# Chunked linear attention feeding a SiLU MLP: the recurrence of the tiled chunks goes from steps of 128 tokens to steps of 64

## The chip, the cores and the metric

One core of one Trainium2 chip. The metric is the device time of one execution in microseconds (us); three runs of the kernel before gave 206.91, 207.03 and 207.21, median 207.03 us. Profile times are counted from the start of the profiled span.

## The reference, cut to what matters

Four batches, eight heads, 768 tokens, head size 64. Attention without softmax and with a decay per head, computed block by block of 64 tokens with a running 64x64 state per head; its output, as 3072 rows of 512, goes through a two-layer MLP with a SiLU.

```
for b in range(nb):                       # blocks of 64 tokens
    intra = (qb @ kb.T * Dmask) @ vb      # Dmask: lam ** (i - j), 0 above the diagonal
    inter = (qb * lam ** (pos + 1)) @ kv_state
    out[b] = intra + inter
    kv_state = lam ** 64 * kv_state + (kb * lam ** (63 - pos)).T @ vb
...
h = x @ w_in                              # x: 3072 x 512, w_in: 512 x 2048
out = (h * sigmoid(h)) @ w_out            # w_out: 2048 x 512
```

The kernel doesn't keep the decay in the state: q is multiplied by a power of lambda, k by its inverse (tables `lam_fwd`, `lam_bwd` by position in the sequence), so that the state is a plain sum and the mask is 0 or 1. The sum may then be cut into blocks of any size.

## The kernel before, in words

**Chunks, pairs, groups.** The 3072 tokens are 24 chunks of 128, six to a batch (`NB`). Heads go in four pairs p of two heads j. Two chunks make a group of 256 columns for the MLP; there are 12 groups. Chunks 0 to 5 (batch 0) are done by other code, in the first 49 us, which the change doesn't touch. Chunks 6 to 23 go through `section`, which is called 12 times, between pieces of the MLP.

**What a section does.** `section(outs, scores, states, ...)` computes, for three lists of chunks, in one burst on TensorE: the *outputs* (score times v, name `op<-ss,vb`, and state times q, `op<-qt,kvs`), the *scores* (`sp<-qt,kn`) and the *states* (`kv_ps<-vb,kb`). Every product is 64x64 weights on one quarter of the array. The quarter, or tile, is (r, x): rows half r (which half of the contraction: tokens 0 to 63 or 64 to 127 of a chunk, or one head of the pair) and columns half x (which half of the output's partitions). For outputs, x is set by `at[p]`, which says for each pair whether its two heads lie straight or crosswise.

Because a chunk is 128 tokens and causal, the products with the first 64 keys have 128 moving columns (queries 0 to 127), those with the last 64 keys have 64. State times q has 128 columns, the state products 64.

**The order within a section** is made by a small list planner at L491-L562: a FIFO of products for each of the four tiles, in which a 64-column product is counted at 32 and a 128-column one at 56, and the emitted order is that of the planned start. FIFOs of row half 0: out of pairs 0-1, scores, states, out of pairs 2-3; of row half 1: states, out of pairs 2-3, scores, out of pairs 0-1. Two row halves may not write one PSUM bank at once, so each bank has a leading row half (`leads`, L539), and the other one starts `LAG` = 220 after the leader's last product there, behind a semaphore (L554-L558). Here "turn" means that hand-over.

After the products: output copies PSUM to `xt` (VectorE or ScalarE), masking of the scores (VectorE, L579: two row ranges times two heads for each chunk, so 4 instructions a chunk), and per chunk of states one addition into `total` and one cast to `kvs` (VectorE, L588, L589).

**Order on the engines.** Nothing is rescheduled: each engine executes its instructions in the order in which the Python code emits them. Before a chunk's v can be used, ScalarE casts it to bf16 (`vcast`, `vb<-vf`, L185), in the same queue as the SiLU of the MLP (L610). POOL scales q and k (`scaled`, L355), SP's queue loads and transposes them.

**Where the 12 sections stand** (main loop, L801-L830). An MLP group g has 8 units of the first product (`ffn1_two`, PSUM tag `h`, 2 banks, one SiLU each) and 8 units of the second (`downs`). Section 1 (score of chunk 6) comes before unit 2 of group 2, right behind `vcast(6)`. Sections 2 and 4 (groups 2 and 3) come before unit 6 of the first product. Sections 3 and 5 to 12 come before unit 6 of the second product of groups 2 to 10. Sections 5 to 11 compute scores of two chunks, sections 6 to 12 outputs of two. `vcast(d)`, for the second chunk d of the next group, comes in unit 1 of the second product when g < 4.

| section | first start, us | outs | scores | states |
|---|---|---|---|---|
| 1 | 51.02 | - | 6 | - |
| 2 | 55.04 | 6 | 7 | 6 |
| 3 | 62.85 | 7 | 8 | 7 |
| 4 | 70.77 | 8 | 9 | 8 |
| 5 | 78.63 | 9 | 10, 11 | 9, 10 |
| 6 | 93.80 | 10, 11 | 12, 13 | 12 |
| 7 | 109.11 | 12, 13 | 14, 15 | 13, 14 |
| 8 | 124.43 | 14, 15 | 16, 17 | 15, 16 |
| 9 | 139.86 | 16, 17 | 18, 19 | 18 |
| 10 | 155.17 | 18, 19 | 20, 21 | 19, 20 |
| 11 | 170.49 | 20, 21 | 22, 23 | 21, 22 |
| 12 | 185.90 | 22, 23 | - | - |

The last chunk of a batch (11, 17, 23) needs no state, and the first one (6, 12, 18) reads none.

Of the kernel before, what the change touches and what calls it, by code (L numbers as in the profile page):

```python
# [7 lines left out]
F32 = mybir.dt.float32  # L8
BF16 = mybir.dt.bfloat16
AF = mybir.ActivationFunctionType  # L10
AL = mybir.AluOpType

BLK = 128
# [25 lines left out]
def kernel(  # L39
# [10 lines left out]
    nc = tc.nc  # L50
    B, H, S, D = q.shape
    assert (B, H, S, D) == (4, 8, 768, 64)
    NB = S // BLK
# [150 lines left out]
    cell = {}  # L204
# [150 lines left out]
    def scaled(c, raw, table, name):  # L355
        dst = nat.tile([128, NP, 2, D], BF16, name=name, tag=name, bufs=6 if name == "kb" else 4)
        src, by = raw.pop(c).rearrange("s (p j) d -> s p j d", j=2), decay(table, c % NB)
        if c < NPAD:
            nc.gpsimd.tensor_tensor(dst, src, by, op=AL.mult)
            return dst  # L360
        nc.gpsimd.tensor_tensor(dst[:, :3], src[:, :3, ::-1, :], by[:, :3, ::-1, :], op=AL.mult)  # L361
        nc.gpsimd.tensor_tensor(dst[:, 3:], src[:, 3:], by[:, 3:], op=AL.mult)
        return dst

    def prep_k(c):
# [115 lines left out]

    at = [(1, 0), (1, 0), (1, 0), (0, 1)]
    LAG = 220

    def section(outs=(), scores=(), states=(), e="AA", tags=(("att", 3),) * 2, spare=None):

        jobs = {(r, x): [] for r in range(2) for x in range(2)}  # L491

        def add(r, x, key, lhsT, rhs, dst, start=False):
            jobs[r, x].append((key, rhs.shape[-1], lhsT, rhs, dst, start))

        n = len(outs)
        if outs:
            ops = [psum.tile([128, 2, n, BLK], F32, name="op", tag=t, bufs=b, padded_shape=[128, 2, 2, BLK]) for t, b in tags]
        states = [c for c in states if c % NB < NB - 1]
        if states:  # L500
            kv = psum.tile([128, len(states), NP, D], F32, name="kv_ps", tag="kv", bufs=1, padded_shape=[128, 2, NP, D])
        sps = {}
        for c in scores:
            for j in range(2):
                t, b = spare if spare and not sps else ("att", 3)
                sps[c, j] = psum.tile([128, NP, BLK], F32, name="sp", tag=t, bufs=b)

        def out(r, i):
            first = {0, 1} if r == i else set()
            for w, c in enumerate(outs):  # L510
                vb, qt = natb[c][2], tr[c][0]
                for p in (2 * i, 2 * i + 1):
                    for j in range(2):
                        x = at[p][j]
                        add(r, x, i, vb[half[r], p, x, :], st[c][j][half[r], p, 64 * r:], ops[i][half[x], p % 2, w, 64 * r:], x in first)
                        first.discard(x)
                    if c % NB:
                        x = at[p][r]
                        add(r, x, i, kvb[c][half[r], p, :], qt[half[r], p, :], ops[i][half[x], p % 2, w, :])

        def state(r):
            for w, c in enumerate(states):
                kb, vb = natb[c][1:]
                for p in range(NP):
                    for j in range(2):
                        add(r, j, "kv", kb[half[r], p, j, :], vb[half[r], p, at[p][j], :], kv[half[j], w, p, :],
                            r == 1 and w == 0 and p == 0)

        def score(r):
            for c in scores:  # L530
                qs, kt = tr[c]
                for p in range(NP):
                    for h in range(2):
                        add(r, h, "s", kt[half[r], p, half[h]], qs[half[r], p, 64 * h:], sps[c, r][half[h], p, 64 * h:], True)

        out(0, 0), score(0), state(0), out(0, 1)
        state(1), out(1, 1), score(1), out(1, 0)

        leads = {"kv": 1, 0: 0, 1: 1}  # L539
        free, done, last = {k: 0.0 for k in jobs}, {}, {}  # L540

        def begin(k):
# [7 lines left out]
        while any(jobs.values()):  # L550
            k = min((k for k in jobs if jobs[k]), key=lambda k: (begin(k), k))
            t = begin(k)
            key, cols, lhsT, rhs, dst, start = jobs[k].pop(0)
            if leads.get(key, k[0]) != k[0] and key in last:  # L554
                turn = nc.tensor.nop()
                tc.add_manual_dep(turn.ins, last.pop(key).ins.name,
                                  mybir.DependencyInfo(mybir.DependencyClass.Sync, mybir.DependencyReason.DATA),
                                  reason="row tiles of one bank")  # L558
            ins = nc.tensor.matmul(dst, lhsT=lhsT, rhs=rhs, start=start, stop=True, skip_group_check=True)  # L559
            free[k] = t + (32 if cols == 64 else 56)  # L560
            if leads.get(key) == k[0]:
                done[key], last[key] = max(free[k], done.get(key, 0)), ins  # L562

        def copy_out():
            for w, c in enumerate(outs):
                x = new_xt(c)
            if n == 2:
                x = xt[group_of[c][0]]
            for i, op in enumerate(ops):
                move(e[i], x[:, 2 * i:2 * i + 2, :], op.rearrange("d p w s -> d p (w s)"))  # L570

        if outs:
            copy_out()
        for c in scores:
            st[c] = [work.tile([128, NP, BLK], BF16, name="ss", tag="ss") for j in range(2)]
            for rows, cols in ((half[0], half[0]), (slice(0, 128), half[1])):
                m = mask[rows, cols]
                for j, ss in enumerate(st[c]):
                    nc.vector.tensor_tensor(ss[rows, :, cols], sps[c, j][rows, :, cols],  # L579
                                            m[:, None, :].to_broadcast([m.shape[0], NP, 64]), op=AL.mult)  # L580
        for w, c in enumerate(states):
            b = c // NB
            kvs = nat.tile([128, NP, D], BF16, name="kvs", tag="kvs", bufs=4)
            if c % NB == 0:
                total[b] = nat.tile([128, NP, D], F32, name="total", tag="total", bufs=2)
                nc.vector.tensor_copy(total[b], kv[:, w])
            else:
                nc.vector.tensor_tensor(total[b], total[b], kv[:, w], op=AL.add)  # L588
            nc.vector.tensor_copy(kvs, total[b])  # L589
            kvb[c + 1] = kvs  # L590

    total = {}

    gt = {}
# [203 lines left out]
    def other():  # L798
        return f"o{1 - otag[0]}", 1

    for g in range(2, len(GROUPS) - 1):  # L801
        c, d, a, b = range(2 * g + 2, 2 * g + 6)
        for i in range(8):
            if g == 2 and i == 2:
                vcast(6)
                section((), (6,))
            if g == 2 and i == 4:
                prep_t(9)
                load_next(2)
            if g < 4 and i == 6:  # L810
                section((c,), (d,), (c,), "DD", (("att", 3), other()))
            ffn1_two(g, i)
        for i, unit in enumerate(downs(g)):
            if i == 1:
                vcast(d) if g < 4 else None
                vcast(a)
            if i == 2:
                if g > 2:
# [4 lines left out]
                vcast(b)  # L823
            if i == 6:
                if g == 2:
                    section((d,), (a,), (d,), "AA", (("att", 3), other()))
                else:
                    cs = [x for x in (a, b) if x < NCHUNK]
                    section((d,) if g == 3 else (c, d), cs, (d, a) if cs else (d,), "AD", (("h", 2),) * 2, other())
            ffn2(*unit)  # L830
    g = len(GROUPS) - 1
    for i in range(8):
# [34 lines left out]
```

## Time and profile before

| what | value |
|---|---|
| median of three runs | 207.03 us (206.91 to 207.21) |
| the profiled execution's own time | 207.43 us |
| its span, first to last instruction | 205.7 us |
| TensorE busy | 197.1 us, 96% of the span |
| VectorE, ScalarE, POOL busy | 86.3, 88.1, 54.7 us |
| tiled products of sections (L559) | 936, busy 14.04 us in all |
| DMA | 38.64 MB, mean 188 GB/s |

"Busy" of TensorE is the union of its instructions' times, and a product's time includes the passage through the array, so that a dense stream overlaps itself: a 128x512 product is shown with 379 ns while the next starts 216 ns after it. Starts are what to compare. Some matmul records are missing (346 of the second product's 368 at L643): in the timeline the first one behind a section is, where eight weight loads stand beside seven products.

### The profile page before, as it was taken

The numbers are of one execution on the slowest core, as the hardware profiler recorded it, in microseconds if no ns is written. First come the engines' busy times: TensorE is split into PE (matmuls) and PEld (weight loads), VectorE is DVE, ScalarE is ACT, GpSimd is POOL, SyncE is SP. The second block draws the span as 40 slices with busy tenths as digits, with TensorE's granted clock in tenths as the row PEclk, the third lists the DMA queues.
The fourth block names the chain that finished last, engine by engine and source line by source line (L and its number), as shares of the span: only waits on it lengthen the run. The fifth ranks groups of instructions, "written<-read, shape, count | busy, mean of one in ns | idle before, by whom it ended". The sixth has DMA issues, their size and how long they took to land.

```text
span 205.7 us, 5525 instructions
## 1 busy us (share of the span) xinstructions
PE 197.1 (96%) x2331; PEld 132.5 (64%) x2354; DVE 86.3 (42%) x202; ACT 88.1 (43%) x159; POOL 54.7 (27%) x96
## 2 busy tenths in 40 slices
PE   7789999999999999999999999999999999999994
PEld 2457544567856855856856856856856856856854
DVE  3898557384446055505405514515315415412011
ACT  2677673323642650641641641641641641621610
POOL 5270001744634507606606063161000000000000
PEclk9999999999999999999999999999999999999999
DMA  3999999998959769969949696999998101101102
GB/s 95 332 353 389 394 407 285 326 223 178 275 110 212 168 127 250 188 154 212 200 99 270 102 267 131 137 285 103 391 197 285 51 0 54 54 0 53 54 0 102
DMA packets 95577, 38.64 MB, mean 188 GB/s; under 512 B 80960, under 2 KB 88512, under 8 KB 95552
## 3 DMA queue, kind: packets, MB, share of 16 engines
q1 hardware_dynamic: 92288, 37.50, 72.1%
q10 hardware_dynamic: 3264, 0.79, 1.8%
q8 instruction: 18, 0.29, 0.6%
q14 instruction: 7, 0.06, 0.1%
HBM read 27.27 MB, written 6.29 MB: 163 GB/s over the span
## 4 chain that ended last, share of the span: by engine, by line
PE 92%; SPq 2%; DMA 2%; issue 1%; POOL 1%; DVE 0%
PE o_ps L643 38%; PE h_ps L605 36%; PE h_ps L699 5%; PE op L559 4%; SPq L231 2%; DMA pair<-in_k_dram 2%; PE sp L559 2%; PE o_part L663 2%; PE kv_ps L559 1%; PE kv_ps L337 1%; PE op L317 1%; PE op L478 1%; POOL kp L260 1%; PE sp L452 0%; PE op L312 0%
## 5 line engine op out<-in xcount | busy, mean ns | idle before, releaser
L643 PE MATMUL o_ps<-w_out_bf,g 128*128 128x512 bf16 x346 | 80.7, 379 | 2.1 <-issue 1.4
L605 PE MATMUL h_ps<-xt,w_in_bf 128*128 128x256 bf16 x672 | 75.9, 273 | 0.0
L605 PEld LDWEIGHTS <-w_in_bf 128*128 128x128 bf16 x672 | 65.5, 98 | 10.1
L610 ACT ACTIVATE g<-h_ps 128x512 bf16<-128x512 f32 x84 | 49.8, 597 | 42.1 <-PE h_ps L605 42.0
L643 PEld LDWEIGHTS <-g 128*128 128x128 bf16 x368 | 35.0, 98 | 38.2
L361 POOL TENSOR_TENSOR qb<-qf,lam_fwd 128x384 bf16<-128x384 f32 x18 | 14.9, 828 | 50.8 <-DMA qf<-in_q_dram 39.4
L185 ACT ACTIVATE xt<-op 128x256 bf16<-128x256 f32 (+1 forms) x16 | 7.7, 504 | 44.8 <-issue 24.8
L649 DVE COPY ob<-o_ps 128x512 f32<-128x512 f32 x11 | 7.6, 688 | 46.0 <-PE o_ps L643 46.0
L579 DVE TENSOR_TENSOR ss<-sp,mask 64x256 bf16<-64x256 f32 (+1 forms) x72 | 24.7, 405 | 2.9 <-PE sp L559 2.9
L189 DVE CAST xt<-op 128x256 bf16<-128x256 f32 (+1 forms) x14 | 7.7, 558 | 27.5 <-PE op L559 27.5
L649 DVE COPY pair<-o_ps 128x512 f32<-128x512 f32 x12 | 8.2, 687 | 21.1 <-PE o_ps L643 20.7
L361 POOL TENSOR_TENSOR kb<-kf,lam_bwd 128x384 bf16<-128x384 f32 x18 | 14.9, 829 | 7.0 <-DMA kn<-kb 4.9
L559 PE MATMUL op<-ss,vb 64*64 64x64 bf16 (+1 forms) x288 | 12.5, 207 | 0.0
L559 PEld LDWEIGHTS <-vb 64*64 64x64 bf16 x288 | 9.4, 108 | 4.3 <-issue 4.2
L699 PE MATMUL h_ps<-xt,w_in_bf 128*128 128x512 bf16 x48 | 10.5, 379 | 0.0
L185 ACT ACTIVATE vb<-vf 128x512 bf16<-128x512 f32 x18 | 10.3, 621 | 0.0
L559 PE MATMUL op<-qt,kvs 64*64 64x128 bf16 x120 | 9.2, 218 | 0.0
L699 PEld LDWEIGHTS <-w_in_bf 128*128 128x128 bf16 x48 | 4.7, 97 | 5.5
L708 ACT ACTIVATE g<-h_ps 128x512 bf16<-128x512 f32 x12 | 6.5, 596 | 3.4 <-PE h_ps L699 3.4
L559 PE MATMUL sp<-qt,kn 64*64 64x128 bf16 (+1 forms) x288 | 7.9, 206 | 0.0
L559 PE MATMUL kv_ps<-vb,kb 64*64 64x64 bf16 x240 | 7.8, 195 | 0.0
L352 POOL TENSOR_TENSOR qb<-pair,lam_fwd 128x512 bf16<-128x512 f32 x2 | 2.0, 1042 | 20.0 <-DMA pair<-in_q_dram 20.0
(91 smaller groups left out, 142.8 us busy)
## 6 DMA issues: line engine op xcount, KB each, us to landing
kf<-in_k_dram SPq DMA_DIRECT2D x19, 256.0 KB, 4.3
vf<-in_v_dram SPq DMA_DIRECT2D x19, 256.0 KB, 4.5
qf<-in_q_dram SPq DMA_DIRECT2D x17, 256.0 KB, 4.2
pair<-in_moe_w_out_dram SPq DMA_DIRECT2D x8, 512.0 KB, 8.0
pair<-in_moe_w_in_dram SPq DMA_DIRECT2D x6, 512.0 KB, 7.4
out_dram<-pair SPq DMA_DIRECT2D x12, 256.0 KB, 3.2
out_dram<-ob SPq DMA_DIRECT2D x11, 256.0 KB, 2.0
pair<-in_k_dram SPq DMA_DIRECT2D x4, 256.0 KB, 4.7
```

Of the source, the lines that this page charges most:

```text
L185: nc.scalar.activation(dst, src, AF.Copy)
L189: nc.vector.tensor_copy(dst, src)
L231: nc.sync.dma_start(out=dst[c][:, lo:hi].rearrange("p h r d -> p h (r d)"), in_=src[b, lo:hi, blk * BLK:(blk + 2) * BLK, :].rearrange("h ( ...
L361: nc.gpsimd.tensor_tensor(dst[:, :3], src[:, :3, ::-1, :], by[:, :3, ::-1, :], op=AL.mult)
L559: ins = nc.tensor.matmul(dst, lhsT=lhsT, rhs=rhs, start=start, stop=True, skip_group_check=True)
L579: nc.vector.tensor_tensor(ss[rows, :, cols], sps[c, j][rows, :, cols], m[:, None, :].to_broadcast([m.shape[0], NP, 64]), op=AL.mult)
L605: nc.tensor.matmul(hps[g, i][:, a:a + 256], lhsT=w_in_bf[:, ko, m * 128:(m + 1) * 128], rhs=xt[g][:, ko, :], start=(ko == 0 and u == 0), s ...
L610: nc.scalar.activation(gg.rearrange("p u n -> p (u n)"), hps[g, i], AF.Silu)
L643: nc.tensor.matmul(o, lhsT=gt[g, ko][:, mt * BLK:(mt + 1) * BLK], rhs=w_out_bf[:, ko, :], start=(ko == 0), stop=(ko == KO_OUT - 1))
L649: nc.vector.tensor_copy(ob, o)
L699: nc.tensor.matmul(hps["m", m], lhsT=w_in_bf[:, ko, m * 128:(m + 1) * 128], rhs=xall[0][:, :, ko, :], start=(ko == 0), stop=(ko == KO_IN - 1))
L708: nc.scalar.activation(gg, hps["m", m], AF.Silu)
```

## The change

It affects `section`, its call sites, and the split of POOL's scaling.

- **Half chunks.** The states argument becomes a list of (chunk, half). Each half of 64 tokens adds to the running sum by itself, and each half's queries read the sum as it stood before that half (`kvh[c, h]`). So a score or score-times-v product covers one half against itself only: all of them have 64 columns. State times q becomes two products of 64 columns. The number of products goes from 936 to 1104: 168 more, all of the two kinds that touch the state.
- **Which states when.** `steps` gives a section the halves up to the first half of the last chunk that it scores: section 1 has (6,0), section 2 (6,1) and (7,0), section 3 (7,1) and (8,0), section 4 (8,1) and (9,0), section 5 (9,1) (10,0) (10,1) (11,0), and so on; second halves of the last chunk of a batch are dropped. Before, a section had the states of its output chunk and the one behind.
- **Banks.** Scores of two chunks share one bank per row half (two banks instead of four). With two halves of the same parity, the states of the two row halves get a bank each and need no turn; with fewer they share one, with a turn.
- **Crosswise pairs.** `at` becomes crosswise in pairs 0 and 2 and straight in 1 and 3, and POOL's scaling is split by even and odd pairs instead of the first three and the last.
- **VectorE.** One mask instruction per row half for all scores of a section (two instead of 4 or 8); an addition and a cast for each half (33 instead of 15 of each); two copies of a 64-column mask in section 1.
- **Casts.** `vcast(d)` moves from the second product to just ahead of sections 2 and 4.

```diff
-        nc.gpsimd.tensor_tensor(dst[:, :3], src[:, :3, ::-1, :], by[:, :3, ::-1, :], op=AL.mult)
-        nc.gpsimd.tensor_tensor(dst[:, 3:], src[:, 3:], by[:, 3:], op=AL.mult)
+        nc.gpsimd.tensor_tensor(dst[:, 0::2], src[:, 0::2, ::-1, :], by[:, 0::2, ::-1, :], op=AL.mult)
+        nc.gpsimd.tensor_tensor(dst[:, 1::2], src[:, 1::2], by[:, 1::2], op=AL.mult)
...
-    at = [(1, 0), (1, 0), (1, 0), (0, 1)]
+    at = [(1, 0), (0, 1), (1, 0), (0, 1)]
...
+        states = [(c, h) for c, h in states if (c + 1) % NB or not h]
+        ns = max([sum(h == x for _, h in states) for x in range(2)])
+        shared = ns < 2
+        if scores:
+            sps = [more("sp", [128, len(scores), NP, D]) for _ in range(2)]
         if states:
-            kv = psum.tile([128, len(states), NP, D], F32, name="kv_ps", tag="kv", bufs=1, padded_shape=[128, 2, NP, D])
+            kv = [psum.tile([128, 2, NP, D], F32, name="kv_ps", tag="kv", bufs=1)]
+            if not shared:
+                kv.append(more("kv_ps", [128, 2, NP, D]))
...
-                        add(r, x, i, vb[half[r], p, x, :], st[c][j][half[r], p, 64 * r:], ops[i][half[x], p % 2, w, 64 * r:], x in first)
+                        add(r, x, i, vb[half[r], p, x, :], st[c][j][half[r], p, :], ops[i][half[x], p % 2, w, half[r]], x in first)
                         first.discard(x)
-                    if c % NB:
-                        x = at[p][r]
-                        add(r, x, i, kvb[c][half[r], p, :], qt[half[r], p, :], ops[i][half[x], p % 2, w, :])
+                for h in range(2):
+                    if (c, h) in kvh:
+                        for p in ps:
+                            x = at[p][r]
+                            add(r, x, i, kvh[c, h][half[r], p, :], qt[half[r], p, half[h]], ops[i][half[x], p % 2, w, half[h]])
...
-                        add(r, h, "s", kt[half[r], p, half[h]], qs[half[r], p, 64 * h:], sps[c, r][half[h], p, 64 * h:], True)
+                        add(r, h, f"s{r}", kt[half[r], p, half[h]], qs[half[r], p, half[h]], sps[r][half[h], w, p, :], True)
...
+    def steps(*cs):
+        return [(c, h) for c, h in [(cs[0] - 1, 1)] + [(c, h) for c in cs for h in range(2)] if c > 5][:-1]
...
             if g == 2 and i == 2:
                 vcast(6)
-                section((), (6,))
+                section((), (6,), steps(6))
...
             if g < 4 and i == 6:
-                section((c,), (d,), (c,), "DD", (("att", 3), other()))
+                vcast(d)
+                section((c,), (d,), steps(d), "DD", (("att", 3), other()))
...
             if i == 1:
-                vcast(d) if g < 4 else None
                 vcast(a)
...
                 if g == 2:
-                    section((d,), (a,), (d,), "AA", (("att", 3), other()))
+                    section((d,), (a,), steps(a), "AA", (("att", 3), other()))
...
-                    section((d,) if g == 3 else (c, d), cs, (d, a) if cs else (d,), "AD", (("h", 2),) * 2, other())
+                    section((d,) if g == 3 else (c, d), cs, steps(*cs) if cs else (), "AD", (("h", 2),) * 2, other())
```

## The prediction

> **What bounds the kernel now.** I read the page's busy times and its chain first, then the waits with TensorE as the waiting engine, then the timeline of one section, last ScalarE's timeline around sections 1, 2 and 4.
>
> ```profile
> span 205.7 us, 5525 instructions
> PE 197.1 (96%) x2331; PEld 132.5 (64%) x2354; DVE 86.3 (42%) x202; ACT 88.1 (43%) x159; POOL 54.7 (27%) x96
> PEclk9999999999999999999999999999999999999999
> PE o_ps L643 38%; PE h_ps L605 36%; PE h_ps L699 5%; PE op L559 4%; SPq L231 2%; DMA pair<-in_k_dram 2%; PE sp L559 2%; PE o_part L663 2%; PE kv_ps L559 1%; PE kv_ps L337 1%; PE op L317 1%; PE op L478 1%; POOL kp L260 1%; PE sp L452 0%; PE op L312 0%
> ```
> ```profile
> PE o_ps L643 <- issue: 1.4, 9, 0.2
> PE warm_ps L213 <- DVE zero L119: 1.3, 1, 1.3
> PE tk L276 <- DVE kp L189: 1.1, 1, 1.1
> ```
> TensorE is the chain, at full granted clock, and after the first 16 us it waits for no other engine. The nine 0.16 us of "issue" lie behind sections 3 and 5 to 12, where the first dense product has no record, and are no wait. So each nanosecond that a section's burst takes more or less is a nanosecond of the end, and a new wait of TensorE counts in full.
>
> **What a section costs.** Section 8, TensorE's timeline:
>
> ```profile
> 124.44 0.25 PE L559 MATMUL kv_ps<-vb,kb 64*64 64x64 bf16 x4
> 124.52 0.23 PE L559 MATMUL kv_ps<-vb,kb 64*64 64x64 bf16 x4
> 124.59 0.23 PE L559 MATMUL kv_ps<-vb,kb 64*64 64x64 bf16 x4
> ...
> 124.68 0.22 PE L559 MATMUL sp<-qt,kn 64*64 64x128 bf16 x1
> 124.74 0.22 PE L559 MATMUL sp<-qt,kn 64*64 64x128 bf16 x1
> 124.79 0.22 PE L559 MATMUL sp<-qt,kn 64*64 64x128 bf16 x1
> 124.85 0.22 PE L559 MATMUL sp<-qt,kn 64*64 64x128 bf16 x1
> ...
> 126.09 1.67 PE L643 MATMUL o_ps<-w_out_bf,g 128*128 128x512 bf16 x7 [0.16 <-issue]
> ```
> The four scores are one tile's, 56 ns apart. Each row of four states is two products on each of two tiles, so 32 ns a step and tile (124.52 to 124.59 for two). The four tiles run beside each other. A section therefore lasts as long as its busiest tile: the sum of 56s and 32s in it. Check, busiest tile before, less its last step, plus 24 ns that the first step is always longer (80 instead of 56): section 7 1208 - 56 + 24 = 1176, first to last start measured 1178; section 8 1264, measured 1280; section 11 1264, measured 1261; sections 5, 6 and 9 come 57, 31 and 30 ns above. The mean excess of sections 5 to 11 is 19 ns. From the last start to the next dense product it is 148 ns where that is recorded (sections 2 and 4); the last product has 128 columns, and I take 124 with 64.
>
> **Part 1: all tiled products at 64 columns, crosswise pairs alternating.** Steps for one tile after, all 32 ns: a chunk's scores 4, score times v 4, state times q 2 per half, a half's states 4 on the two tiles of its row half. Before, the three equal pairs of `at` gave tiles (0,1) and (1,0) three of four state-times-q products of 56; now all are even. Two-chunk section 8: 8 + 8 + 8 + 8 steps = 1024, where the busiest tile had 1296. Turns cost nothing there: bank 0's leader ends at 256 and bank 1's at 512, the followers start at 768, over 220 behind. Sections 2 to 4 share a state bank: leader done at 128, follower not before 348, though its scores are done at 256 (224 in section 2); a restart after an idle turn costs 20 more (first steps of 52 instead of 32 in section 3). Section 12 has 256 + 220 + 256 = 732 and 44 of restarts, as now (planned last start 964, measured 1008).
>
> | section | busiest tile before | last start measured | busiest after, with turns | last start after | saved, with 24 of the exit |
> |---|---|---|---|---|---|
> | 3 | 648 | 673 | 604 | 616 | 81 |
> | 5 | 1000 | 1025 | 768 | 760 | 289 |
> | 6, 9 | 1168 | 1167, 1166 | 1024 | 1016 | 175, 174 |
> | 7, 10 | 1208 | 1178, 1178 | 960 | 952 | 250, 250 |
> | 8, 11 | 1296 | 1280, 1261 | 1024 | 1016 | 288, 269 |
> | 12 | 784 | 1008 | 732 | 744 | 288 |
>
> Sum 2.06 us; less 7 times the 19 ns excess 1.93 us. The trace has no stretch with all four tiles at 64 columns, which asks for a start each 8.0 ns. Counted over the trace's starts, the best 16 successive ones are 7.9 ns apart on average, the best 32 8.9, the best 64 9.6; all of these have a tile with 128 columns among them, so they needn't be a limit. Bounds: 8.0, nothing more; 9.6, sections 5 to 11 with 96, 120, 120, 128, 120, 120, 128 products take 1.26 us more. I take 8.0, since the 16 show it.
>
> A rule speaks against this part: the Trainium skill, "TensorE: Matmul & The Clock Gate", section "Wait — 56ns, not 53.3ns?", says that start-to-start of matmuls never falls below about 25 ns, however few columns. The rows above show 7.9 ns across tiles, and 32 on one tile; taken across tiles, the rule would make section 8 last 128 x 25 = 3.2 us, an estimate from that page, and the change cost over 10 us; I go by the rows.
>
> **Part 2: states earlier, a new wait in three sections.** Before, a section's states were of a chunk whose v had been cast long ago. Now sections 1, 2 and 4 have states of chunk 6, 7 and 9, and the cast stands just ahead of them in ScalarE's queue, behind the SiLU of the MLP unit that TensorE has only just finished.
>
> ```profile
> 49.63 1.13 ACTq L239 DMA_DIRECT2D vf<-in_v_dram  x1
> 50.81 1.09 ACT L610 ACTIVATE g<-h_ps 128x512 bf16<-128x512 f32 x2 [1.70 <-PE h_ps L605]
> 51.78 0.63 ACT L185 ACTIVATE vb<-vf 128x512 bf16<-128x512 f32 x1
> ...
> 55.15 0.60 ACT L610 ACTIVATE g<-h_ps 128x512 bf16<-128x512 f32 x1 [0.28 <-PE h_ps L605]
> ...
> 70.88 0.60 ACT L610 ACTIVATE g<-h_ps 128x512 bf16<-128x512 f32 x1 [0.22 <-PE h_ps L605]
> ```
> TensorE's starts follow the emitted order to a few ns in every section, so what is emitted behind a waiting product waits too.
> - Section 1 starts at 51.02; its states come after 4 steps of scores, at 51.17. Chunk 6's cast already runs at 51.78 to 52.41 (two SiLUs are late behind a DMA issue). Release 49 ns later (the SiLU that ends at 51.407 lets a product go at 51.456), four state steps 0.12, exit 0.12: next dense product at 52.70, measured 51.456. **+1.25 us.**
> - Section 2, T = 55.04: the SiLU of unit 5 runs from T + 0.11 to T + 0.70, the cast starts 0.1 before a predecessor's end (51.78 against 51.90) and takes 0.62 to 0.63: release at T + 1.28. The states of (7,0) were due at about T + 0.42. Behind them still 4 + 3 steps less one (0.21) and the exit 0.12: T + 1.615, before T + 0.78. **+0.83 us.**
> - Section 4, T = 70.77: the same, with 4 + 4 steps: T + 1.65, before T + 0.82. **+0.83 us.**
>
> Sum +2.91 us. What queues behind is the rest of the MLP, which has no slack. The landing of v is not late (chunks 6, 7, 9 landed at 45.1, 48.3, 58.5), nor is POOL's k (48.8 and 58.9 for 7 and 9). A pause of 1.1 us (the third row of waits) left the granted clock at full, so I add nothing for it. Bounds: 0 if the casts came in time, 2.91 + 0.3 if the restarts after such a pause are slower. In sections 3 and 5 to 11 the casts come before: they run at 119.85 for section 8, at 124.43.
>
> **Part 3: the rest, at nothing.** VectorE: after section 8 now 0.69 (xt) + 8 x 0.34 (masks) + 2 x 0.77; after, 0.69 + 2 x 0.69 (as the 128x512 masks at L457, 686 ns) + 4 x 0.77 = 5.2 us, with 15 us to the next section; the output copy behind it is 0.3 us later, its bank is wanted 7 us after the section. In section 1 two small mask copies, two masks and the state's copy and cast, some 2 us, end before section 2. xt is copied first as now, 0.8 us before the MLP wants it (126.8 against 127.6). POOL: 828 + 402 ns become two of 128x256, between these 0.6 each; bounds 2 x 0.40 and 2 x 0.83, and POOL scales a chunk over 5 us before its section. Fewer score banks: none is short. If the covers failed, TensorE would wait up to some 0.3 us a section.
>
> **Sum.** +2.91 - 1.93 = +0.98 us: 207.43 becomes 208.4 us for the profiled execution. That lies 0.40 above the median; for the median 207.03 + 0.98 = **208.0 us**.
>
> **Rivals.**
> - *The casts don't hold TensorE up* (faster). Then sections 1, 2 and 4 change by +0.03, -0.07 and -0.08, and the time is 207.03 - 1.93 - 0.12 = 205.0. The point: `vb` must be ready by T + 0.42 in sections 2 and 4. For it speaks ScalarE's idle 0.28 us before each SiLU, and that v landed 7 us before; against it, that a cast emitted after unit 5 can't start before that unit's SiLU, which itself ends at T + 0.70. Chance 8%.
> - *Starts can't come each 8 ns* (slower). At 9.6 ns: 208.0 + 1.26 = 209.3. For it: averages rise with the length of the stretch; against: 7.9 over 16. 14%.
> - *Waits half as long* (no change): one of the three casts earlier, or excesses gone: +0.4 or less, 207.4. 12%.
> - *The bursts don't shrink at all*, turns or LDWEIGHTS taking over: 207.03 + 2.9 = 209.9. For it nothing but that no row shows it; 4%.
>
> Forecast 62%. Measurement tells 0.2% (0.41 us) from no change. Faster 8%, within 12%, slower 80% (forecast, second and last rival). The range leaves out the faster rival, the last one and the far end of the others: 207.3 to 209.3.
>
> **What would show it.** In the profile after: TensorE waits for ScalarE three times, 0.8 to 1.3 us, at sections 1, 2 and 4; sections 5 to 11 last 0.76 to 1.05 us from first to last start; 1104 tiled products. Wrong if no wait on ScalarE appears (205), or if section 8 lasts 1.2 us or more (209).

## The result and the profile after

The kernel after takes 209.45 us (median of six runs, 209.24 to 211.27), the kernel before 207.23 in the same job (six runs, 206.91 to 207.86). The ratio is 1.0119, 95% interval 1.0081 to 1.0158: slower by about 1.2%, and beyond the upper end of the prediction's range. Ratios here and below leave out single runs that took over 1.5% longer than the fastest of their kernel. The profiled execution takes 209.37 us, 1.94 more than the one of before.

The page of after: span, busy times, clock, the chain by line.

```profile
span 207.5 us, 5877 instructions
PE 198.4 (96%) x2522; PEld 131.8 (64%) x2522; DVE 88.0 (42%) x190; ACT 88.2 (42%) x159; POOL 54.9 (26%) x96
PEclk9999999999999999999999999999999999999999
PE 90%; DMA 2%; ACT 2%; SPq 2%; ACTq 1%; POOL 1%; issue 0%; DVE 0%
```

And its waits of TensorE: us in total, times, the longest.

```profile
PE kv_ps L580 <- ACT vb L185: 3.1, 3, 1.6
PE warm_ps L213 <- DVE zero L119: 1.3, 1, 1.3
PE tk L276 <- POOL kp L260: 0.8, 1, 0.8
```

The first line is new: in three sections the state products (the tiled line is now L580) wait for the cast of v. ScalarE and its issuing queue (ACTq) stand in the chain now; before, it read

```profile
PE 92%; SPq 2%; DMA 2%; issue 1%; POOL 1%; DVE 0%
```

The clock is granted in full, so the difference is time that TensorE stood still or spent otherwise, not a slower clock.

Section by section, from first start to the next dense product (148 ns behind the last start before, from the sections where that product has a record; 125 to 143 after, where all have one), the spans differ like this:

| sections | predicted, us | measured, us |
|---|---|---|
| 1, 2, 4: waits | +1.25, +0.83, +0.83 = +2.91 | +1.25, +0.83, +0.82 = +2.90 |
| 3 | -0.08 | +0.04 |
| 5, 8, 11 | -0.29, -0.29, -0.27 | -0.19, -0.15, -0.21 |
| 6, 9 | -0.18, -0.17 | -0.08, -0.02 |
| 7, 10 | -0.25, -0.25 | -0.14, -0.07 |
| 12 | -0.29 | -0.25 |
| bursts, sum | -1.93 (2.06 less the excess of 0.13) | -1.07 |
| all | +0.98 | +1.83 (span: 207.5 - 205.7) |

For section 1 the number is when the next dense product starts (52.70 against 51.456). The section itself began 0.50 us earlier than before, at 50.52, and the wait swallowed that: counted from its own start it lost 1.74.

So one half of the sum came out to 0.01 us and the other half is 0.86 us short. The sections add up to the difference of the spans, so nothing is left for the dense work around them. Another 0.1 lies around the span. The medians differ by 2.2 and the profiled executions by 1.9; the remaining 0.3 has no place in one profile. And 0.2 of the distance to the forecast of 208.0 is its base: it was added to 207.03, and the kernel before takes 207.23 here.

**Where the waits come from.** ScalarE's timeline of after around sections 1 and 2: start, duration, instruction, in brackets the idle time before it.

```profile
49.24 1.52 ACTq L239 DMA_DIRECT2D vf<-in_v_dram  x1
50.81 1.08 ACT L635 ACTIVATE g<-h_ps 128x512 bf16<-128x512 f32 x2 [2.19 <-PE h_ps L630]
51.78 0.63 ACT L185 ACTIVATE vb<-vf 128x512 bf16<-128x512 f32 x1
...
56.41 0.60 ACT L635 ACTIVATE g<-h_ps 128x512 bf16<-128x512 f32 x1 [0.28 <-PE h_ps L630]
56.90 0.62 ACT L185 ACTIVATE vb<-vf 128x512 bf16<-128x512 f32 x1
```

TensorE's timeline of section 2, which starts at 56.30:

```profile
56.55 0.29 PE L580 MATMUL sp<-qt,kn 64*64 64x64 bf16 x8
57.57 0.22 PE L580 MATMUL kv_ps<-vb,kb 64*64 64x64 bf16 x2 [0.73 <-ACT vb L185]
...
57.91 0.50 PE L630 MATMUL h_ps<-xt,w_in_bf 128*128 128x256 bf16 x3
```

The cast starts when the SiLU ahead of it has all but ended and ends at 57.52; the states of chunk 7 start at 57.57, 1.27 after the section's start (predicted 1.28). In section 1 the cast runs at 51.78 to 52.41, as before: the wait is the length by which TensorE is ahead of it.

**Where the bursts are long.** Section 8 of after, TensorE's timeline; each line with x2 is two products, on the two tiles of one row half, so two such lines are a round of the four tiles:

```profile
127.16 0.20 PE L580 MATMUL kv_ps<-vb,kb 64*64 64x64 bf16 x2
127.19 0.20 PE L580 MATMUL op<-qt,kvs 64*64 64x64 bf16 x2
127.19 0.20 PE L580 MATMUL kv_ps<-vb,kb 64*64 64x64 bf16 x2
127.22 0.20 PE L580 MATMUL op<-qt,kvs 64*64 64x64 bf16 x2
127.22 0.20 PE L580 MATMUL kv_ps<-vb,kb 64*64 64x64 bf16 x2
...
127.52 0.20 PE L580 MATMUL kv_ps<-vb,kb 64*64 64x64 bf16 x2
127.54 0.20 PE L580 MATMUL sp<-qt,kn 64*64 64x64 bf16 x2
127.56 0.20 PE L580 MATMUL kv_ps<-vb,kb 64*64 64x64 bf16 x2
127.57 0.20 PE L580 MATMUL sp<-qt,kn 64*64 64x64 bf16 x2
127.59 0.20 PE L580 MATMUL kv_ps<-vb,kb 64*64 64x64 bf16 x2
...
128.04 0.28 PE L580 MATMUL op<-qt,kvs 64*64 64x64 bf16 x8
128.25 0.61 PE L668 MATMUL o_ps<-w_out_bf,g 128*128 128x512 bf16 x2
```

At first the lines of one row half are 32 ns apart (127.16, 127.19, 127.22), later 33 to 34 (127.52, 127.56, 127.59). Around the two turns, at products 95 and 100 (counted from 0), a start comes 17 and 26 ns after the one before instead of 8; so it does, 16 to 18 and 25 ns after, at products 47 and 52 and at 109 and 114, where there is no turn. The last start comes 1.136 us after the first, where the plan had 0.992 and the prediction, with the longer first step, 1.016. The second half of the experiments is about the reason.

### The profile page after: what moved, and what is told of

Same layout as the page of the kernel before. It is cut to its first block, busy times and chain, and to the rows that moved or that the text cites. A ratio compares the mean times of both kernels' runs of the same rounds, so it can differ in the third digit from the quotient of the medians.

```text
span 207.5 us, 5877 instructions
## 1 busy us (share of the span) xinstructions
PE 198.4 (96%) x2522; PEld 131.8 (64%) x2522; DVE 88.0 (42%) x190; ACT 88.2 (42%) x159; POOL 54.9 (26%) x96
## 4 chain that ended last, share of the span: by engine, by line
PE 90%; DMA 2%; ACT 2%; SPq 2%; ACTq 1%; POOL 1%; issue 0%; DVE 0%
PE o_ps L668 38%; PE h_ps L630 35%; PE h_ps L724 5%; PE op L580 3%; DMA pair<-in_k_dram 2%; SPq L231 2%; PE o_part L688 2%; PE kv_ps L580 1%; PE sp L580 1%; ACT g L635 1%; ACTq L239 1%; PE kv_ps L337 1%; ACT vb L185 1%; PE op L317 1%; PE op L478 1%; POOL kp L260 1%
## 5 line engine op out<-in xcount | busy, mean ns | idle before, releaser
L668 PE MATMUL o_ps<-w_out_bf,g 128*128 128x512 bf16 x368 | 83.9, 379 | 0.0
L630 PEld LDWEIGHTS <-w_in_bf 128*128 128x128 bf16 x672 | 65.4, 98 | 10.0
L635 ACT ACTIVATE g<-h_ps 128x512 bf16<-128x512 f32 x84 | 49.8, 597 | 43.9 <-PE h_ps L630 43.9
L361 POOL TENSOR_TENSOR qb<-qf,lam_fwd 128x256 bf16<-128x256 f32 x18 | 11.1, 615 | 53.6 <-DMA qf<-in_q_dram 33.5
L361 POOL TENSOR_TENSOR kb<-kf,lam_bwd 128x256 bf16<-128x256 f32 x18 | 11.1, 615 | 7.2 <-PE kv_ps L580 6.3
L600 DVE TENSOR_TENSOR ss<-sp,mask 128x512 bf16<-128x512 f32 (+1 forms) x22 | 11.9, 584 | 2.4 <-PE op L580 1.4
L612 DVE TENSOR_TENSOR total<-total,kv_ps 128x256 f32<-128x256 f32 x30 | 12.5, 418 | 0.8
L613 DVE CAST kvs<-total 128x256 bf16<-128x256 f32 x33 | 11.2, 339 | 1.1
L580 PE MATMUL kv_ps<-vb,kb 64*64 64x64 bf16 x264 | 8.3, 196 | 3.1 <-ACT vb L185 3.1
L362 POOL TENSOR_TENSOR kb<-kf,lam_bwd 128x256 bf16<-128x256 f32 x18 | 11.2, 624 | 0.0
L362 POOL TENSOR_TENSOR qb<-qf,lam_fwd 128x256 bf16<-128x256 f32 x18 | 11.1, 618 | 0.0
L580 PEld LDWEIGHTS <-vb 64*64 64x64 bf16 x288 | 7.4, 105 | 4.4 <-issue 4.2
L580 PE MATMUL op<-ss,vb 64*64 64x64 bf16 x288 | 9.9, 198 | 0.1
L580 PE MATMUL op<-qt,kvs 64*64 64x64 bf16 x264 | 9.5, 194 | 0.0
```

The costliest lines, as they stand in the source:

```text
L361: nc.gpsimd.tensor_tensor(dst[:, 0::2], src[:, 0::2, ::-1, :], by[:, 0::2, ::-1, :], op=AL.mult)
L362: nc.gpsimd.tensor_tensor(dst[:, 1::2], src[:, 1::2], by[:, 1::2], op=AL.mult)
L600: nc.vector.tensor_tensor(ss, sp.rearrange("k w p q -> k (w p) q"), cell["m"][:, None, :].to_broadcast([128, len(scores) * NP, D]), op=AL. ...
L612: nc.vector.tensor_tensor(total[b], total[b], place(c, h), op=AL.add)
L630: nc.tensor.matmul(hps[g, i][:, a:a + 256], lhsT=w_in_bf[:, ko, m * 128:(m + 1) * 128], rhs=xt[g][:, ko, :], start=(ko == 0 and u == 0), s ...
L635: nc.scalar.activation(gg.rearrange("p u n -> p (u n)"), hps[g, i], AF.Silu)
```

## Experiments

Theory: the waits are the casts' place ahead of sections 2 and 4 and behind ScalarE's DMA issue in section 1, and cost 2.9 us; the bursts save half of what was counted because TensorE can't start a product each 8.0 ns for that long, and because turns aren't free. Rivals: the bursts' dense work around them became slower; the step of a tile is more than 32 ns; the bank of the states or the planner's numbers hold the bursts up; the pauses come from elsewhere.

### The casts on VectorE, earlier

Kernel after, with the casts of v for chunks 6, 7 and 9 taken off ScalarE's queue and emitted one or two units earlier:

```diff
+            if g == 2 and i == 1:
+                vcast(6, "D")
+            if g < 4 and i == 4:
+                vcast(d, "D")
             if g == 2 and i == 2:
-                vcast(6)
...
-                vcast(d)
```

> The kernel after, with the casts of v of chunks 6, 7 and 9 on VectorE one or two MLP units earlier (VectorE is idle there). Theory (three waits on ScalarE's cast cost 1.25 + 0.83 + 0.82 = 2.90 us and nothing else was lost): no wait of TensorE on a cast; sections 1, 2 and 4 last about as long as before (within 0.05 us each), sections 5 to 12 as in the kernel after; some 1.0 us faster than the kernel before, 206.2 against 207.2. Rival (TensorE would wait for something else there, such as masks, state sums or SiLU): at least one of sections 1, 2, 4 keeps 0.3 us or more, and the time is 207 or above.

Measured: 207.03 us (12 runs) against 207.49 (29 runs), ratio 0.9977, 0.9958 to 0.9995. The profiled execution takes 206.57, span 204.9. Its waits:

```profile
PE o_ps L668 <- issue: 1.5, 9, 0.2
PE warm_ps L213 <- DVE zero L119: 1.3, 1, 1.3
PE tk L276 <- POOL kp L260: 0.8, 1, 0.8
```

No cast is waited for (the first line is the missing records again). TensorE's last product starts at 201.38, 3.18 us earlier than in after (204.56); the span is only 2.7 shorter, because the last output is issued on SP's queue for longer in this execution (1.73 us for the last two instead of 1.24). Sections 2 and 4 last 0.702 and 0.781 us from first to last start, instead of 1.486 and 1.518. Three casts moved by one or two units take back the whole loss; what is left of the change is a gain of about 0.2%. Sections 5 to 11 last 0.843, 1.107, 1.060, 1.135, 1.081, 1.108 and 1.075 us: within 1 ns of after but for sections 9 and 10, which had 1.170 and 1.127 there, so the missing half of the saving has nothing to do with the casts.

### The casts on ScalarE, earlier

The same, but on ScalarE:

```diff
+            if g == 2 and i == 1:
+                vcast(6)
+            if g < 4 and i == 4:
+                vcast(d)
             if g == 2 and i == 2:
-                vcast(6)
...
-                vcast(d)
```

> The kernel after, with the same three casts left on ScalarE, but emitted one unit (chunk 6) or two units (7 and 9) earlier. Theory (the place in ScalarE's queue decides): no wait in sections 2 and 4, as the SiLU behind the cast is late by 0.25 us where the section gives it 0.8; section 1 still waits for the cast, which comes behind the late SiLU of unit 0, by 0.7 to 0.8 us instead of 1.25; about 0.2 us faster than before, 207.0. Rival (ScalarE has no room for a cast inside the first product's units): the wait moves to the MLP's units, TensorE waits for a SiLU 0.3 us or more in each group, 207.6 or more.

Measured: 207.51 (10 runs), ratio 1.001, 0.9985 to 1.0035; span 205.3. The waits are as expected, the time is not 207.0. One wait is left:

```profile
PE kv_ps L580 <- ACT vb L185: 0.5, 1, 0.5
```

It is section 1's, 0.73 us start to start. ScalarE's timeline there:

```profile
49.34 0.87 ACTq L239 DMA_DIRECT2D vf<-in_v_dram  x1
50.26 0.60 ACT L635 ACTIVATE g<-h_ps 128x512 bf16<-128x512 f32 x1 [1.59 <-PE h_ps L630]
50.76 0.62 ACT L185 ACTIVATE vb<-vf 128x512 bf16<-128x512 f32 x1
```

The DMA issue ends at 50.21, the SiLU of unit 0 runs behind it, and the cast behind that, until 51.38; the section starts at 50.57. Sections 2 and 4 wait for nothing. So it is the place in the queue that cost the time in those two, not ScalarE as an engine, and in section 1 it is what stands ahead in the queue. That execution also has gaps of 0.11 to 0.14 us in sections 8 to 10, at places where no wait is listed; these three sections last 0.34 us longer together than with the casts on VectorE.

### The moved cast alone

Kernel before, with `vcast(d)` ahead of sections 2 and 4 and nothing else changed:

```diff
             if g < 4 and i == 6:
+                vcast(d)
                 section((c,), (d,), (c,), "DD", (("att", 3), other()))
...
             if i == 1:
-                vcast(d) if g < 4 else None
```

> The kernel before with only the move of the casts of chunks 7 and 9 to just ahead of sections 2 and 4. Theory (the cast costs only because a product now needs it): no change, within 0.1 us of 207.2. Rival (the cast at this place costs by itself, by delaying the SiLUs and with them the MLP's banks): 0.3 to 0.6 us slower.

Measured: 207.36, ratio 1.0003, 0.9977 to 1.003. The late cast costs nothing while no product of that section needs it; the loss is made by the late cast and the earlier states together. (The profiled execution, at 209.27 us the longest of the ten, isn't used: k's transposes landed late in it, two waits of 1.9 us in all. The others took 206.90 to 208.08.)

### Long bursts, all kinds in one place

Kernel before, with six bursts of products that nobody reads in group 10: 64, 32 and 128 moving columns, four or two tiles, 256 products each and one of 64.

```diff
+    bursts = {1: (256, 64, 4), 2: (256, 32, 4), 3: (256, 128, 4), 4: (256, 64, 2), 5: (256, 32, 2), 6: (64, 64, 4)}
...
+        for n in range(count):
+            r, x = order[n % tiles]
+            nc.tensor.matmul(banks[r][half[x], :cols], lhsT=zero[half[r], half[x]], rhs=zero[half[r], :cols],
...
```

> The kernel before with six bursts of 64x64 products on a zero tile, written to unused banks, ahead of units 1 to 6 of group 10's first product: 256 of 64 columns on four tiles, 256 of 32 columns on four tiles, 256 of 128 columns on four tiles, 256 of 64 columns on two tiles, 256 of 32 columns on two tiles, 64 of 64 columns on four tiles. Theory of an issue limit (one product with its weight load each 8.3 ns once a backlog is used up): mean distance of starts in the later part 8.3 ns for 64 and for 32 columns on four tiles, 14 for 128 columns, 16 for 64 columns on two tiles. Rival, the tile's step itself grows when four run: 8.3 for 64 columns, but below 6 for 32 columns on four tiles, and 8 to 9 for 32 columns on two. In the burst of 64 products the first 40 or so would come at 8.0 and the rest at 8.3 by the first theory.

Measured: 241.92 us. It disturbed itself. TensorE's timeline in it, and below it the rows of two windows with PEclk as the third number from the right:

```profile
196.32 2.21 PE L808 MATMUL burst<-zero 64*64 64x64 bf16 x128 [0.72 <-issue]
200.05 1.83 PE L808 MATMUL burst<-zero 64*64 64x64 bf16 x104 [1.52 <-issue]
```
```profile
160.00:176.00 16.00, 15.48 (x366) 10.77 (x367) 6.52 (x17) 6.07 (x11) 0.00 (x0) 1.00 0.10 39
179.50:189.70 10.20, 7.79 (x314) 6.23 (x315) 0.00 (x0) 1.20 (x2) 0.00 (x0) 0.50 0.02 5
```

TensorE stood still eight times for 0.3 to 2.0 us without a semaphore, six times 128 products (256 instructions with their weight loads) after the pause before, and after the longest of these pauses the granted clock was 0.50 for some 10 us. The page's instruction queue moves packets of some 16 KB (19 of them, 0.31 MB, in after); that 256 instructions are one packet is the reading that fits, not more. So the burst of 32 columns on four tiles ran at half clock and said nothing. What can be used: 64 columns on four tiles 7.9 ns a start for the first 64 and then 8.3; 64 or 32 columns on two tiles 15.8; 128 columns on four tiles 13.9 to 14.0.

### One short burst a group

The same idea with 120 products, one burst in each of groups 5 to 9, between units of the first product and away from the sections; each form ran once. Weights by columns 64x64, 32x32, 64x64 with two turns, 32 weight columns by 64, 64 by 32.

> The kernel before with one burst of 120 products on a zero tile ahead of unit 3 of groups 5 to 9, on four tiles in turn, into unused banks: 64 weight and 64 moving columns; 32 and 32; 64 and 64 with two turns (a wait on a product 48 places back) ahead of products 56 and 88; 32 weight and 64 moving columns; 64 weight and 32 moving columns. Theory of an issue limit: after some 45 to 64 products the distance of starts is 8.3 ns in all five, and 32 x 32 is no faster in that part, though 4 to 5 ns apart before it; each turn costs 15 to 30 ns more. Rival, the tile step itself grows to 33 when four run: 32 x 32 stays well below 8 ns to its end, and turns cost nothing beyond the wait.

Measured, from TensorE's timeline (the first four; the second number is until the last product has left the array):

```profile
99.69 1.18 PE L814 MATMUL burst<-zero 64*64 64x64 bf16 x120
116.36 1.37 PE L814 MATMUL burst<-zero 64*32 64x32 bf16 x120
133.17 1.23 PE L814 MATMUL burst<-zero 64*64 64x64 bf16 x120
149.81 1.15 PE L814 MATMUL burst<-zero 64*32 64x64 bf16 x120
```

| weight columns, moving columns | start to start at first, ns | later, ns | first to last start, ns |
|---|---|---|---|
| 64, 64 | 7.9 to 8.0 for 60 products | 8.4 | 983 |
| 64, 64 with two turns | 7.9 for 44 | 8.4 | 1034 |
| 32, 64 | 7.2 to 7.4 for 38 | 8.4 | 955 |
| 32, 32 | 6.2 to 6.4 for 32 | 8.2 to 8.9, apart from pauses | 1189, with two pauses of 80 |
| 64, 32 | 7.9 for 96 | 8.3 | 969 |

Two things follow. The tile's step of 32 ns is right for 64 weight columns (64 by 32 is no faster than 64 by 64): the rival "step over 32 ns" falls. And behind the first few dozen products every form ends at 8.3 to 8.4 ns a product or above, whatever the tiles could take. Three of the forms get there the sooner the quicker they go (32, 38, 60 products). A stock of weight loads and products, gathered during the dense work, that runs out, and then the rate at which new ones come, would look like that; no run shows the stock itself, and 64 by 32, no quicker than 64 by 64, gets there only after 96. Two turns, 32 products apart, cost 51 ns. The Trainium skill's floor, about 25 ns start to start ("TensorE: Matmul & The Clock Gate", section "Wait — 56ns, not 53.3ns?"), fits here for one tile with 32 weight and 32 moving columns (four tiles at 6.2 to 6.4 make 25 to 26 ns a tile), and not for the array as a whole.

### Waits in the burst

128 products of 64x64 in groups 5 to 9, each burst once: plain; eight of them with a wait for VectorE that is already met; eight such waits for VectorE and eight for POOL; two turns; all of these. (VectorE's writes ended 0.14 to 0.31 us before the product that waits for them, not long before as the expectation says; POOL's ended 15 us and more before.)

> The kernel before with one burst of 128 products (64x64 on all four tiles) ahead of unit 4 of groups 5 to 9; the products go to spare banks and nothing reads them. Group 5: plain. Group 6: eight of the products wait for a VectorE instruction that ended long before. Group 7: eight weight loads wait so for POOL as well. Group 8: two turns, that is two waits of TensorE on a product 48 places earlier. Group 9: both kinds of waits and two turns. First to last start, from the rows of the bursts apart (7.9 ns for some 60 products, then 8.4; two turns cost 51 ns there): plain 127 x 8.2 = 1.04 us; theory (the waits of a section cost time by themselves): groups 6 and 7 longer by 8 to 25 ns for each wait, 0.06 to 0.2 us or 0.13 to 0.4 us, group 9 by 0.2 to 0.4 us; rival (a wait that is already met costs nothing, and what the sections of the changed kernel lose beyond the start limit and the turns is supply of instructions): groups 6 and 7 within 20 ns of group 5, groups 8 and 9 longer by 0.05.

First to last start 1.369, 1.049, 1.368, 1.100 and 1.100 us. TensorE's timeline, plain and with two turns (in windows of their own):

```profile
100.14 1.58 PE L822 MATMUL burst<-zero 64*64 64x64 bf16 x128
```
```profile
152.16 1.29 PE L822 MATMUL burst<-zero 64*64 64x64 bf16 x128
```

The plain burst is the slow one: pauses of 129 and 184 ns behind its 75th and 127th product, with no semaphore in it. Eight met waits for VectorE cost nothing (1.049, and 1.04 was the sum for none), two turns 51 ns, and with sixteen waits on top again the same 1.100. The burst with both kinds of waits and no turns lost 0.32 us in small pieces from its 78th product on. They come every eight products, as the waits do, but go on at products 112 and 120, behind the last wait, and the same waits were free in the last burst. So a met wait for VectorE alone costs nothing, a turn costs 25 ns here, and whether the waits have a part in that burst's loss is open. The pauses of the plain burst are a third thing: it has no waits behind its third product.

### A state bank for each row half

The casts on VectorE as above, and in sections 2 to 4 a bank of its own for each row half's states, so that their turn goes:

```diff
-        shared = ns < 2
+        shared = ns < 2 and not spare
...
-                section((c,), (d,), steps(d), "DD", (("att", 3), other()))
+                section((c,), (d,), steps(d), "DD", (("att", 3), other()), (f"o{otag[0]}", 1))
...
```

> e1 (casts early, on VectorE), and in sections 2 to 4 a PSUM bank for the states of each row half, so that the states need no turn there. Theory (the stall of 141 ns in each of these sections is that turn, a wait that holds up all four tiles): first to last start falls from 0.70, 0.73 and 0.78 us to 0.56 to 0.65, where the turn of the outputs' bank is next; 0.2 to 0.4 us less in all, 206.1 against 207.2 for before. Rival (the 141 ns are the arrival of k or v of the new chunk, or of instructions): the stall stays.

Measured: 206.75 (9 runs, one of them 342.91), ratio 0.9965, 0.9945 to 0.9984. Section 3 lasts 0.727 us instead of 0.734, section 4 0.701 instead of the 0.781 with the shared bank; both were expected at 0.56 to 0.65. After had a pause there, between these two lines of TensorE's timeline,

```profile
65.22 0.26 PE L580 MATMUL sp<-qt,kn 64*64 64x64 bf16 x6
65.43 0.22 PE L580 MATMUL kv_ps<-vb,kb 64*64 64x64 bf16 x2
```

of 141 ns. It is gone, but the outputs' bank has a turn too and now ends last, with a pause of 91 ns at 0.516 in section 3: that turn takes 353 ns from the leader's last start to the follower's first, where the plan and the prediction had 252 (a step of 32 and 220 behind its end). The theory that one bank is what section 3 lacks falls; what is left there is the length of a turn that nothing fills. In section 4 the bank was worth 0.08 us. Section 2 of this profile waits for k's transpose:

```profile
PE sp L580 <- DMA kn<-kb: 0.8, 1, 0.8
```

### The planner told the measured numbers

The last kernel with `T64` 33.4 instead of 32 and `LAG` 270 instead of 220, by which the list planner orders the products.

> e6 with the planner's numbers set to what sections showed: 33.4 for a product and 270 for a turn, in place of 32 and 220. Theory (the order hardly depends on them, since all tiles are even): within 0.1 us of e6. Rival (products wait because the planned order puts a turn too early): 0.3 us or more faster than e6.

Measured: 206.63 (5 runs), ratio 0.9967, 0.9942 to 0.9992; within 0.12 of the kernel above, as the theory says; sections 3 to 12 differ from those of that kernel by -0.11 to +0.07 us, without a pattern. Better numbers for the planner return nothing that can be measured.

### Crosswise pairs alone

Kernel before with only `at` alternating and POOL's split by even and odd pairs; everything else, 128-column products too, as it was.

```diff
...
-    at = [(1, 0), (1, 0), (1, 0), (0, 1)]
+    at = [(1, 0), (0, 1), (1, 0), (0, 1)]
```

> The kernel before with only the alternating crosswise pairs and POOL's split by even and odd pairs. Theory (a section lasts as long as its busiest tile where starts are 9 ns or more apart): tile (0,0) gets two products of 56 more for each chunk with a state to read, so sections 3 and 4 last 0.04 us longer, 5 0.04, 6 and 9 0.08, 7 and 10 0.06, 8 and 11 0.08; section 12 0.2 shorter, since row half 0's first bank is done sooner; together 0.3 us slower, 207.5. Rival (the number of products sets the length, not the busiest tile): no section changes by more than 0.02 us.

Measured: 207.39, ratio 1.0003, 0.9987 to 1.0018. Sections 3 to 11 get longer by 0.02 to 0.08 us, the way that the busiest tile says (6 and 9 by 0.05 where it said 0.08), and section 12 shorter by 0.19: together +0.22 us, too little to tell in the time. Alternating alone gains nothing; that it pays with the 64-column halves follows from the sums of the tiles, no run has the halves without it.

## Why the prediction was right in half and wrong in half

- **What bounds.** Right. TensorE is the chain before and after, and each wait put on it counted in full: 2.90 us added at sections 1, 2 and 4, and 1.58, 0.78 and 0.74 returned there when the casts moved (0.33 of it because section 1 is reached earlier in that execution than in the one of before).
- **Part 2, the new waits.** Right: +2.91 counted, +2.90 measured; with the casts elsewhere they are gone, with the casts late but the states not early they cost nothing in the time. The sign was decided here. Two rivals, that the casts don't hold TensorE up and that the waits are half as long, fall in the waits of after. That section 1 came out to 0.00 is partly luck: the cast ran at 51.78 in both executions because ScalarE's last DMA issue ended at 50.76 in both, and in that of the casts on ScalarE, earlier, it ended at 50.21.
- **Part 1, the bursts.** This is the failed step: -1.93 counted, -1.07 measured, so the saving was put too high by 0.86. The way was right (the rival that the bursts don't shrink at all falls), and no section of after is shorter than its busiest tile; but the prediction let nothing else add to it, and three terms were mis-sized.
  - *"I take 8.0, since the 16 show it"*: 16 starts are a shorter stretch than the 60 that a plain burst makes at 7.9 before it falls to 8.4 (the 16 are products 55 to 71 of section 5, which had come slowly until then). A burst of 128 takes 1.049 us first to last instead of 1.016, one of 120 0.983 instead of 0.952, some 30 ns a section, 0.2 us in seven.
  - *"Turns cost nothing there"*: two turns cost 51 ns in a burst by itself. In the sections, where they stand 2 products apart (in 6 and 9, 14), they cost about 26 together: section 11 has no other step and lasts 1.075 us, 26 ns more than the burst of 128; section 10 of the kernel with its own state banks lasts 1.008, 25 ns more than the burst of 120. That is 0.18 us in seven. In sections 3 and 12, where nothing fills the turns, the forecast missed by 0.12 and 0.04: a turn took 0.36 and 0.28 us from start to start instead of 0.25.
  - What the prediction had no term for: further steps of the same size where no turn stands. Sections 8 and 11 have the same list of products. By how much each starts behind its planned start, in ns (turns ahead of products 96 and 98):

| product, counted from 0 | 48 | 56 | 92 | 104 | 116 | last |
|---|---|---|---|---|---|---|
| section 8 | 17 | 35 | 47 | 77 | 107 | 144 |
| section 11 | 17 | 16 | 21 | 51 | 55 | 83 |

  Both lose 30 ns at the turns (4 of them drift); section 8 alone loses 18 near product 52 and 30 near 112. Such steps stand in sections 5 to 9, and sections 9 and 10 have pauses of 84 and 110 ns as well, all without a wait that the profile shows to end there. The pauses make 0.18 beyond a normal step, the smaller steps the rest, some 0.23.

  Together with two exits (last start to next dense product) of 143 for 124 ns, 0.04: 0.20 + 0.18 + 0.16 + 0.18 + 0.23 + 0.04 = 0.99, less the mean excess of 0.13 that the prediction had already allowed, 0.86. The 0.23 is what is left over, not a measured sum. So for 0.41, pauses and steps without a turn, the runs show the place and not the cause; the other 0.45 has a named term, whose size is in part carried over from bursts by themselves.
- **The second rival**, that starts can't come each 8 ns, was right in kind and too large: it had 9.6 ns for the whole burst, +1.26 us in sections 5 to 11, whose last starts come 0.79 later than the prediction's table has them, and the rate makes 0.2 of that. Its average over 64 starts, 9.6, had sections with 128-column products among them. In the sections the truth lay between the forecast and this rival; the total of 209.45 is above its 209.3 because the base was 0.2 higher and the medians differ by 0.3 more than the profiles.
- **Part 3, the rest at nothing.** Right. After's groups: POOL's halves, VectorE's masks and states, mean ns behind the busy time, then idle time before them.

```profile
L361 POOL TENSOR_TENSOR kb<-kf,lam_bwd 128x256 bf16<-128x256 f32 x18 | 11.1, 615 | 7.2 <-PE kv_ps L580 6.3
L600 DVE TENSOR_TENSOR ss<-sp,mask 128x512 bf16<-128x512 f32 (+1 forms) x22 | 11.9, 584 | 2.4 <-PE op L580 1.4
L612 DVE TENSOR_TENSOR total<-total,kv_ps 128x256 f32<-128x256 f32 x30 | 12.5, 418 | 0.8
L613 DVE CAST kvs<-total 128x256 bf16<-128x256 f32 x33 | 11.2, 339 | 1.1
L362 POOL TENSOR_TENSOR kb<-kf,lam_bwd 128x256 bf16<-128x256 f32 x18 | 11.2, 624 | 0.0
```

  POOL's halves take 0.62 us (0.6 counted), an addition and a cast 0.42 + 0.34 (0.77 counted), and no wait of TensorE in the sections is for VectorE or POOL.
- **Its own checks.** Three waits on ScalarE: there, at 1.8, 0.9 and 0.9 us start to start, the first longer because its section began earlier. Sections 5 to 11 at 0.76 to 1.05 us: not so, 0.84 to 1.17. Section 8 below 1.2: yes, at 1.136, so the sign that was to go with 209 stayed away and the time came all the same, since every section lost a little. 1104 products: yes.

The pauses without a semaphore stay open. They hit sections 9 and 10 of after, 8 to 10 with the casts on ScalarE, earlier, 7 to 9 with own state banks, and none of before's sections 5 to 11 (the longest step from start to start there is 56 ns); a burst of 128 plain products shows them too, and in long bursts most came 256 instructions apart. That speaks for the supply of instructions and against banks and order, but no run here changed the supply itself. The smaller steps without a turn, and the 0.32 us of the burst with both kinds of waits, are open with them.

## What to carry to other kernels

When a change makes an input wanted earlier, look up where its producer stands in its queue and what it stands behind: here three casts, each 0.6 us long, cost 2.9 us, and emitting them one or two units earlier on an engine with room gave all of it back. Count a dense burst of small products by two limits, the tiles' and the supply's, and take the supply's from a stretch as long as the burst, since the first dozens come faster. A hand-over between row halves costs something even where the follower is due much later (25 ns each in a burst by itself).

The best version, the change with the three casts on VectorE and own state banks, runs at 0.9965 of before (0.9945 to 0.9984), and without the extra banks at 0.9977 (0.9958 to 0.9995): the change without its waits is worth some 0.2 to 0.3%.

## What the runs showed of the hardware

- A weight load with its product came each 8.3 to 8.4 ns once 38 to 60 products (96 with 32 moving columns) of a dense burst on four tiles had gone; before that at the tiles' rate, 7.9 with 64 weight columns, 7.2 to 7.4 with 32. With 32 weight and 32 moving columns it was 6.2 to 6.4 for 32 products, then 8.2 to 8.9.
- A tile's step is 32 ns with 64 weight columns for 64 and for 32 moving columns.
- In runs of hundreds of weight loads and products without a break there were standstills of 0.3 to 2.0 us, most of them 128 products apart, and a granted clock of 0.50 for some 10 us after the longest.
- Waits for VectorE that had been met for 0.14 us or more cost nothing in a burst (eight of them in 1.049 us); a wait for TensorE's own product 48 places back cost 25 ns.
- A turn between the row halves of one bank that nothing fills took 277 to 363 ns from the leader's last start to the follower's first (sections 12 and 3 of after).
